# The last 96 columns of gate and up as one product with tokens stationary, transposed by DMA

## Chip, cores, metric

One core of one Trainium2 chip. The metric is the device time of one execution in microseconds (us), the median of several runs; lower is better. The span in a profile (first to last instruction) is about 1.8 us shorter than the time of the same run. All runs quoted here are fast (none over 1.5% above the fastest run of its kernel).

Engines: PE is TensorE (matmuls), PEld its weight loads, DVE is VectorE, ACT is ScalarE, POOL is GpSimd, SP is the engine that issues most DMAs.

## The reference, cut

Two layers, each a linear attention block and a gated MLP ("GLU"), on 2048 tokens of width 512, hidden width F = 1376. The change touches the GLU alone:

```python
def _B_ref(x, W_gate, W_up, W_down):              # W_gate, W_up: 512 x 1376, W_down: 1376 x 512
    gate = jnp.einsum("bsd,df->bsf", x, W_gate)
    up = jnp.einsum("bsd,df->bsf", x, W_up)
    gate = gate * (lambda x, dt: x.astype(dt))(gate > 0, gate.dtype)
    h = gate * up
    return jnp.einsum("bsf,fd->bsd", h, W_down)
...
x = x + _A_ref(_layernorm(x, axis=-1), A_wqkv, A_w_phi, A_wo)
x = x + _B_ref(_layernorm(x, axis=-1), B_W_gate, B_W_up, B_W_down)
# and both once more
```

## The kernel before

A recording layer notes each operation with what it reads and writes and a guessed duration; a list scheduler orders the operations of each engine, trying several priorities; each DMA gets one of 48 completion semaphores in rotation. 1376 = 10 x 128 + 96, so each GLU has eleven chunks of hidden columns. In all of them the weights are the stationary operand (loaded before the matmul, PEld) and the tokens stream against them, so that the result has hidden columns on partitions, as the down product needs it. The tokens go through in slabs: two slabs of 256 and three of 512 tokens in each layer.

```python
S, D, H, DH, F = 2048, 512, 32, 16, 1376
NT, NSLAB, NC, NFC = 16, 4, 4, 11
FLAST = F - 10 * 128                       # 96
...
def glu_up(self, ts, ring, tag, out, on_act=()):      # ts: the slab's tiles of 128 tokens
    ...
    def step(fc):
        Mf = 128 if fc < 10 else FLAST
        ...
        for bank, W, wr in ((gb, k.Wg, "Wg"), (ub, k.Wu, "Wu")):
            for ic in range(NC):
                op("pe", ... e.matmul(k.pb[bank][0:Mf, 0:n], W[:, ic, fc * 128:fc * 128 + Mf],
                                      k.yT[:, ic, c0:c0 + n], ...) ...)
        op("act", ... e.activation(k.gate_sb[0:Mf, gs, 0:n], k.pb[gb][0:Mf, 0:n], ACT.Relu) ...)
        ...                                           # in some chunks ACT also copies up to SBUF
        op("dve", ... e.tensor_tensor(k.hT[0:Mf, u, 0:n], k.gate_sb[...], ..., ALU.mult) ...)
    for fc in range(NFC):
        out.append(lambda fc=fc: step(fc))
```

Normalised tokens come to yT (all but the first four tiles), and attention outputs to oT, by DMA transposes on the SP queue. Two pieces of the recording layer matter later: how completion semaphores are handed out, and the waits at the very end.

```python
def prepare(self):
    ...
    dma_rr = 0
    for o in order:
        ...
        if o.is_dma:
            stream = ("d", dma_rr % self.n_dma_sems)      # 48 semaphores in rotation
            dma_rr += 1
...
def final_dma_waits(self, eng, dma_sems):                 # on SP, after its last DMA
    for s, c in self.final_counts.items():
        if isinstance(s, tuple) and c:
            eng.wait_ge(dma_sems[s[1]], 16 * c)
```

The softmax here doesn't subtract the row's maximum and nothing guards it: scores larger than these inputs give would overflow.

Of the kernel before, what the change touches and what calls it, by code (L numbers as in the profile page):

```python
# [347 lines left out]
ALU = mybir.AluOpType  # L348
# [20 lines left out]
class Kernel:  # L369
# [10 lines left out]
    def r(self, *key):  # L380
        x = self.R.get(key)
        if x is None:
            x = self.R[key] = Res(str(key), pe_ordered=(key[0] == "pb"))
        return x
# [12 lines left out]
    def alloc(self, E):  # L397
        nc = self.nc

        def sb(name, shape, dt=BF16):  # L400
            t = E(nc.sbuf_tensor(name, [P] + shape, dt))
            setattr(self, name, t)
            return t

        sb("x_sb", [NT, 512])
        sb("yT", [NC, S])
        sb("wv_p", [NC, 512])
        sb("Wqp", [NC, 512])
        sb("Wkp", [NC, 512])
        sb("wo_p", [NC, 512])  # L410
        sb("Wg", [NC, F])
        sb("Wu", [NC, F])
        sb("Wd", [NFC, 512])
        sb("expk", [NT, 2, 512])
        sb("vsb", [NT, NC, 130])
        sb("expq", [NSLAB, NC, 2, 512])
        sb("kvbd", [NG, GW])
        sb("hT", [NHU, 512])
        sb("numbf", [2, NG, GW])
        sb("tsc", [2, 1024])  # L420
        sb("osb", [2, 512])
        sb("oT", [4, NC, 128])
        sb("gate_sb", [3, 512])
        sb("ytile", [4, 512])
        sb("ident", [128])
        sb("mask8", [8])
        sb("mask8t", [8])
        sb("phi_c", [NC, DH])
        sb("stats6", [NT, 6], FP32)
        sb("mv", [NT, 2], FP32)  # L430
        sb("rv1", [NT, 1], FP32)
        sb("rstd", [NT, 1], FP32)
        sb("nmr", [NT, 1], FP32)
        sb("agg", [4, 3], FP32)
        sb("aggw", [2], FP32)
        sb("mhalf", [4, 1], FP32)
        sb("Zk", [2, 64], FP32)
        sb("rZk", [4, 64], FP32)
        sb("zm", [2, 64], FP32)
        sb("zd", [2, 32], FP32)  # L440
        sb("zr", [2, 32], FP32)
        sb("ab", [2, 64])
        self.ps = E(nc.psum_tensor("ps", [P, 8, 512], FP32))
        self.pb = [self.ps[:, i, :] for i in range(8)]
        self.RP = [self.r("pb", i) for i in range(8)]


    def setup(self):
        op, dma, r = self.op, self.dma, self.r
        k = self  # L450
        A_wqkv, A_w_phi, A_wo = self.A_wqkv, self.A_w_phi, self.A_wo
        xv = self.A_x.rearrange("b (t p) d -> p (b t) d", p=P)
        wqkv_v = A_wqkv.rearrange("(c p) n -> p c n", p=P)
        WqT = k.hT[:, 4:8, :]
        wk_n = k.hT[:, 8:12, :]
        BD = k.hT[:, 12, :].rearrange("p (c m) -> p c m", c=NC)
        R_BD = r("hT", 12)
        R_WqT = [r("hT", i) for i in range(4, 8)]
        R_wkn = [r("hT", i) for i in range(8, 12)]

        ones_c = k.tsc[:, 0, 0:128]
        op("pool", lambda e: e.memset(ones_c, 1.0), [], [r("tsc", 0)], 200, "ones")
        op("pool", lambda e: e.affine_select(k.ident[:], ones_c, [[1, 128]], ALU.is_equal, 0.0, base=0, channel_multiplier=-1),
           [r("tsc", 0)], [r("ident")], 300, "ident")
        op("pool", lambda e: e.memset(k.mhalf[:], -0.5), [], [r("mhalf")], 150, "mhalf")
        op("pool", lambda e: e.affine_select(k.mask8t[:], ones_c[:, 0:8], [[-16, 8]], ALU.is_ge, 0.0, base=0, channel_multiplier=1),
           [r("tsc", 0)], [r("mask8t")], 200, "mask8 a")
        op("pool", lambda e: e.affine_select(k.mask8[:], k.mask8t[:], [[16, 8]], ALU.is_ge, 0.0, base=15, channel_multiplier=-1),
           [r("mask8t")], [r("mask8")], 200, "mask8 b")

        n0 = len(self.prog.ops)

        def ldx(t0, t1, after=()):
            dma("sp", lambda e: e.dma_start(k.x_sb[:, t0:t1, :], xv[:, t0:t1, :]), list(after), [r("x", t) for t in range(t0, t1)], 131072 * (t1 - t0) if t1 > t0 + 1 else 96000, f"dma x{t0}")
        dma("sp", lambda e: e.dma_start(k.phi_c[:], A_w_phi.rearrange("(kc hl) d f -> (hl d) kc f", hl=8)), [], [r("phi_c")], 16384, "dma phi")
        for ic in range(NC):
            dma("act", (lambda ic: lambda e: e.dma_start(wk_n[:, ic, :], A_wqkv[ic * 128:(ic + 1) * 128, 512:1024]))(ic), [], [R_wkn[ic]], 96000, f"dma wk{ic}")
        for t in range(4):
            ldx(t, t + 1)
        first = [R_wkn[3]]  # L480
        ldx(4, 8, first)
        dma("sp", lambda e: e.dma_start(k.wv_p[:], wqkv_v[:, :, 1024:1536]), first, [r("wv", ic) for ic in range(NC)], 524288, "dma wv")
        ldx(8, 12, first)
        ldx(12, 16, first)
        o = dma("sp", lambda e: e.dma_start_transpose(WqT, A_wqkv[:, 0:512]), first, R_WqT, 524288, "dma wqT")
        o.dur = 7000.0
        for j, o in enumerate(self.prog.ops[n0:]):
            o.boost = 1e9 - 1e7 * j

        op("pool", lambda e: e.tensor_tensor(  # L490
            BD.rearrange("p c (h f) -> p c h f", f=DH),
            k.phi_c[:].unsqueeze(2).to_broadcast([P, NC, 8, DH]),
            k.mask8[:].unsqueeze(1).unsqueeze(3).to_broadcast([P, NC, 8, DH]), ALU.mult),
           [r("phi_c"), r("mask8")], [R_BD], 1040, "BD")
        op("pool", lambda e: e.memset(k.aggw[:, 0:1], -0.5), [], [r("aggw")], 100, "agg w0")
        op("pool", lambda e: e.memset(k.aggw[:, 1:2], 1.0 / D), [], [r("aggw")], 100, "agg w1")
        op("pool", lambda e: e.memset(k.vsb[:, :, :, 128:130], 1.0), [], [r("vones")], 250, "v ones")
        op("pool", lambda e: e.tensor_copy(k.kvbd[:, :, 136:144], k.mask8[:].unsqueeze(1).to_broadcast([P, NG, 8])), [r("mask8")], [r("kvones")], 230, "kv ones")

    def compose_k(self):  # L500
# [242 lines left out]
    def glu_up(self, ts, ring, tag, out, on_act=()):  # L743
        op, r, k = self.op, self.r, self
        RY = [r("yT", t) for t in ts]
        c0, n = ts[0] * 128, len(ts) * 128
        du = n * 0.42 + 1
        def step(fc):
            Mf = 128 if fc < 10 else FLAST
            gb, ub = next(ring), next(ring)  # L750
            u = self.unit % NHU
            self.unit += 1
            for t in ts:
                self.unit_of[t, fc] = (u, (t - ts[0]) * 128)
            gs = u % 3
            for bank, W, wr in ((gb, k.Wg, "Wg"), (ub, k.Wu, "Wu")):
                for ic in range(NC):
                    op("pe", (lambda bank, W, ic, fc, Mf: lambda e: e.matmul(k.pb[bank][0:Mf, 0:n], W[:, ic, fc * 128:fc * 128 + Mf], k.yT[:, ic, c0:c0 + n], start=(ic == 0), stop=(ic == NC - 1)))(bank, W, ic, fc, Mf),  # L758
                       [r(wr, ic)] + RY, [self.RP[bank]], du, f"{tag} {wr} {ts[0]} {fc} {ic}")
            op("act", (lambda Mf, gb, gs: lambda e: e.activation(k.gate_sb[0:Mf, gs, 0:n], k.pb[gb][0:Mf, 0:n], ACT.Relu))(Mf, gb, gs),  # L760
               [self.RP[gb]], [r("gate", gs)], 170 + n * 0.833, f"{tag} relu {ts[0]} {fc}")
            if fc in on_act:
                tu = 12 + u % 4
                ru = [r("expk", tu, 0), r("phik", tu, 0)]
                op("act", (lambda Mf, ub, tu: lambda e: e.activation(k.expk[0:Mf, tu, 0, 0:n], k.pb[ub][0:Mf, 0:n], ACT.Copy))(Mf, ub, tu),  # L765
                   [self.RP[ub]], ru, 170 + n * 0.833, f"{tag} up {ts[0]} {fc}")
                op("dve", (lambda Mf, tu, gs, u: lambda e: e.tensor_tensor(k.hT[0:Mf, u, 0:n], k.gate_sb[0:Mf, gs, 0:n], k.expk[0:Mf, tu, 0, 0:n], ALU.mult))(Mf, tu, gs, u),  # L767
                   [r("gate", gs)] + ru, [r("hT", u)], 150 + n * 0.535, f"{tag} h {ts[0]} {fc}")
            else:
                op("dve", (lambda Mf, ub, gs, u: lambda e: e.tensor_tensor(k.hT[0:Mf, u, 0:n], k.gate_sb[0:Mf, gs, 0:n], k.pb[ub][0:Mf, 0:n], ALU.mult))(Mf, ub, gs, u),  # L770
                   [r("gate", gs), self.RP[ub]], [r("hT", u)], 150 + n * 1.04, f"{tag} h {ts[0]} {fc}")

        for fc in range(NFC):
            out.append(lambda fc=fc: step(fc))

    def glu_down(self, t, ring, tag, halves=1):
# [195 lines left out]
```

## Time and profile before

| | before |
|---|---|
| median time | 392.31 us (3 runs, 391.47 to 392.65) |
| span of the profile | 390.3 us |
| PE busy | 379.4 us (97%) |
| the chunk of 96 columns on PE | 80 matmuls, 13.9 us by start-to-start times |

From the page of the kernel before: span, busy time by engine, the two queues whose packets the page calls "instruction", here taken as instruction fetches (packets, MB, share of 16 DMA engines), and the engines' shares of the chain that ended last.

```profile
span 390.3 us, 6397 instructions
PE 379.4 (97%) x2331; PEld 208.0 (53%) x2331; DVE 272.0 (70%) x547; ACT 206.6 (53%) x389; POOL 168.5 (43%) x284
...
q8 instruction: 18, 0.29, 0.3%
q14 instruction: 13, 0.11, 0.1%
...
PE 88%; POOL 4%; ACT 3%; DMA 2%; DVE 1%; issue 1%; ACTq 0%; POOLq 0%
```

PE is the bound, and the chain that ended last, on the page below, says the same. Where it has slack is seen by stretches. These are the busy times by window (columns: window, its length, then busy us and count for PE, PEld, DVE, ACT, POOL, granted clock, DMA share, GB/s); the first and last stretch hold the two GLUs:

```profile
72.00:223.00 151.00, 150.88 (x839) 80.04 (x840) 111.31 (x224) 64.03 (x132) 66.78 (x111) 1.00 0.18 35
262.00:378.00 116.00, 116.00 (x660) 62.59 (x659) 64.45 (x140) 54.63 (x120) 30.03 (x62) 1.00 0.19 41
```
```profile
240.00:265.00 25.00, 24.57 (x180) 14.75 (x180) 21.26 (x53) 21.58 (x38) 14.22 (x30) 1.00 0.24 49
```

PE is busy for all but 0.1 us of the two long stretches, so PE time removed there should come off the time. Between 240 and 265 us, where the attention of the second layer goes over into its GLU, 0.4 us is idle even by busy time. Busy time hides small gaps, because the record of a matmul (379 ns for 512 columns) is longer than its step (216 ns). Later sections therefore use "gaps": the start-to-start times of all matmuls, less what each shape takes when nothing is in the way: 216, 109, 62.5 and 56 ns for 512, 256, 144 and up to 129 columns, by the steps in the trace before, and for 192 columns the 83 ns of the forecast.

The groups of matmuls by shape (count, busy us, mean ns, idle before), the chunk first, and below it two shapes with few columns:

```profile
L758 PE MATMUL ps<-yT,Wu 128*96 128x512 bf16 x24 | 9.1, 379 | 0.0
L758 PE MATMUL ps<-yT,Wg 128*96 128x512 bf16 x24 | 8.9, 379 | 0.0
L758 PE MATMUL ps<-yT,Wu 128*96 128x256 bf16 x16 | 3.6, 273 | 0.0
L758 PE MATMUL ps<-yT,Wg 128*96 128x256 bf16 x16 | 3.3, 273 | 0.0
...
L706 PE MATMUL ps<-kvbd,expq 128*128 128x144 bf16 x256 | 35.0, 226 | 0.5 <-ACT numbf L366 0.5
L663 PE MATMUL ps<-vsb,expk 128*128 128x129 bf16 x256 | 19.9, 220 | 1.0 <-POOL expk L634 0.6 <-ACT expq L693 0.3
```

"128*96" says that 96 of the array's columns hold weights; the other chunks have 128*128. All tokens stream all the same: the median step is 216 ns for 512 tokens and 109 for 256 with either form, so the 32 empty columns save no time.

### The profile page before, as it was taken

What the parts mean: (1) busy time and instruction counts of PE and PEld (TensorE: products, weight loads), DVE (VectorE), ACT (ScalarE), POOL (GpSimd) and SP (SyncE); (2) the same over time, 40 slices, a digit from 0 to 9 for tenths busy, and PEclk for the clock granted to TensorE, in tenths of its full rate; (3) what the DMA queues carried; (4) which work ended last, traced back from release to release, by engine and by line L of the source; (5) the groups of instructions that cost most, each with busy time, mean ns of one, the idle gap of its engine ahead of it and who ended that gap; (6) DMA issues with size and microseconds to landing.
All of it is one profiled execution on the core that took longest, in us unless ns stands there. A gap on an engine that the chain in (4) does not pass through costs nothing.

```text
span 390.3 us, 6397 instructions
## 1 busy us (share of the span) xinstructions
PE 379.4 (97%) x2331; PEld 208.0 (53%) x2331; DVE 272.0 (70%) x547; ACT 206.6 (53%) x389; POOL 168.5 (43%) x284
## 2 busy tenths in 40 slices
PE   5999989999999999999999999999999999999997
PEld 3445554667644544444444457567774554444444
DVE  4999978877766888866766777897986776232222
ACT  5898859834633404533453484985563462553340
POOL 5499936641724363372244543584553242100000
DMA  6833682311311322401000110132323132100002
GB/s 179 228 67 71 191 299 53 69 40 32 53 40 27 43 55 44 84 10 28 14 15 0 27 29 3 40 80 57 55 55 69 27 42 67 29 14 27 17 12 67
DMA packets 61663, 23.01 MB, mean 59 GB/s; under 512 B 53472, under 2 KB 60608, under 8 KB 61632
## 3 DMA queue, kind: packets, MB, share of 16 engines
q1 hardware_dynamic: 60912, 22.02, 24.4%
q10 hardware_dynamic: 720, 0.59, 0.5%
q8 instruction: 18, 0.29, 0.3%
q14 instruction: 13, 0.11, 0.1%
HBM read 7.91 MB, written 2.10 MB: 26 GB/s over the span
## 4 chain that ended last, share of the span: by engine, by line
PE 88%; POOL 4%; ACT 3%; DMA 2%; DVE 1%; issue 1%; ACTq 0%; POOLq 0%
PE ps L758 39%; PE ps L785 19%; PE ps L617 7%; PE ps L737 7%; PE ps L690 6%; PE ps L706 4%; PE ps L663 3%; PE ps L648 2%; POOL expk L634 2%; ACT expq L693 2%; DVE stats L551 1%; DMA x_sb<-in_A_x_dram 1%; DMA hT<-in_A_wqkv_dram 1%; ACT expk L620 1%; POOL rstd L576 1%
## 5 line engine op out<-in xcount | busy, mean ns | idle before, releaser
L758 PE MATMUL ps<-yT,Wg 128*128 128x512 bf16 (+3 forms) x440 | 130.1, 337 | 0.5 <-DMA yT<-ytile 0.2
L758 PE MATMUL ps<-yT,Wu 128*128 128x512 bf16 (+3 forms) x440 | 129.6, 336 | 0.0
L760 ACT ACTIVATE gate_sb<-ps 128x512 bf16<-128x512 f32 (+3 forms) x110 | 55.9, 512 | 105.3 <-PE ps L758 102.9
L785 PE MATMUL ps<-Wd,hT 128*128 128x512 bf16 (+2 forms) x363 | 106.8, 373 | 0.0
L634 POOL TENSOR_TENSOR expk<-expk,rZk 128x1024 bf16<-128x1024 bf16 (+1 forms) x32 | 59.5, 1878 | 37.1 <-DVE rZk L631 19.7
L758 PEld LDWEIGHTS ps<-yT,Wg 128*128 128x128 bf16 (+1 forms) x440 | 43.4, 100 | 33.8 <-issue 1.1
L758 PEld LDWEIGHTS ps<-yT,Wu 128*128 128x128 bf16 (+1 forms) x440 | 43.7, 100 | 32.6 <-ACT expk L765 0.2
L767 DVE TENSOR_TENSOR hT<-gate_sb,expk 128x512 bf16<-128x512 bf16 (+3 forms) x73 | 29.8, 409 | 37.9 <-ACT expk L765 33.0
L785 PEld LDWEIGHTS ps<-Wd,hT 128*128 128x128 bf16 (+1 forms) x363 | 35.3, 98 | 36.6 <-DVE x_sb L787 0.6
L551 DVE BATCH_NORM_STATS2 stats<-x_sb 128x6 f32<-128x512 bf16 x64 | 42.6, 682 | 5.5 <-DMA x_sb<-in_A_x_dram 5.1
L366 ACT ACTIVATE numbf<-ps 128x432 bf16<-128x432 f32 x64 | 33.1, 536 | 19.5 <-PE ps L706 19.4
L629 DVE TENSOR_REDUCE Zk<-expk 128x64 f32<-128x1024 bf16 x32 | 37.7, 1194 | 5.7 <-ACT expk L620 5.4
L731 POOL TENSOR_TENSOR osb<-tsc 128x512 bf16<-128x512 bf16 x28 | 32.5, 1162 | 19.9 <-DVE tsc L726 17.8
L737 PE MATMUL ps<-wo_p,oT 128*128 128x512 bf16 x128 | 39.8, 379 | 0.0
L770 DVE TENSOR_TENSOR hT<-gate_sb,ps 128x512 bf16<-128x512 bf16 (+2 forms) x37 | 22.7, 613 | 20.8 <-PE ps L758 19.6
L693 ACT ACTIVATE expq<-ps 128x1024 bf16<-128x1024 f32 (+1 forms) x40 | 32.6, 861 | 7.3 <-PE ps L690 7.0
L765 ACT ACTIVATE expk<-ps 128x512 bf16<-128x512 f32 (+3 forms) x73 | 36.1, 497 | 0.1
L706 PE MATMUL ps<-kvbd,expq 128*128 128x144 bf16 x256 | 35.0, 226 | 0.5 <-ACT numbf L366 0.5
L620 ACT ACTIVATE expk<-ps 128x512 bf16<-128x512 f32 x44 | 23.9, 598 | 21.5 <-PE ps L617 21.2
L690 PE MATMUL ps<-yT,Wqp 128*128 128x512 bf16 x128 | 34.6, 379 | 0.6 <-ACT expq L693 0.5
L787 DVE TENSOR_TENSOR x_sb<-x_sb,ps 128x512 bf16<-128x512 bf16 (+1 forms) x33 | 22.0, 669 | 18.8 <-PE ps L785 18.4
L559 POOL TENSOR_TENSOR rstd<-rv,mhalf 128x1 f32<-128x1 f32 (+1 forms) x53 | 31.9, 607 | 2.9
(73 smaller groups left out, 429.2 us busy)
## 6 DMA issues: line engine op xcount, KB each, us to landing
out_dram<-x_sb SPq DMA_DIRECT2D x15, 128.0 KB, 1.7
x_sb<-in_A_x_dram SPq DMA_DIRECT2D x3, 512.0 KB, 6.2
Wu<-in_B_W_up_dram SPq DMA_DIRECT2D x4, 344.0 KB, 5.9
Wg<-in_B_W_gate_dram SPq DMA_DIRECT2D x4, 344.0 KB, 5.5
Wd<-in_B_W_down_dram SPq DMA_DIRECT2D x5, 256.0 KB, 6.9
yT<-ytile SPq DMA_TRANSPOSE x60, 2.5
hT<-in_A_wqkv_dram ACTq DMA_DIRECT2D x4, 128.0 KB, 3.1
x_sb<-in_A_x_dram SPq DMA_DIRECT2D x4, 128.0 KB, 3.7
```

The lines of the kernel that those rows point to most:

```text
L366: return e.activation(out, in_, ACT.Copy) if hasattr(e, "activation") else e.tensor_copy(out, in_)
L551: op("dve", (lambda t: lambda e: e.bn_stats(k.stats6[:, t, :], k.x_sb[:, t, :]))(t), [r("x", t)], [r("st", t)], 685, f"{tag} stats {t}")
L629: op("dve", lambda e: e.tensor_reduce(k.Zk[:, zb, :], k.expk[:, t, :, :].rearrange("p s (h f) -> p (s h) f", f=16), AX.X, ALU.add), [r("ex ...
L634: op(eng, (lambda s0, s1: lambda e: e.tensor_tensor(k.expk[:, t, s0:s1, :].rearrange("p s (h f) -> p (s h) f", f=16), k.expk[:, t, s0:s1, ...
L690: op("pe", (lambda c, ic, bank: lambda e: e.matmul(k.pb[bank][:], k.Wqp[:, ic, c * 128:(c + 1) * 128], k.yT[:, ic, st * 512:(st + 1) * 512 ...
L693: op("act", (lambda c0, s, b0: lambda e: e.activation(k.expq[:, st, c0:c0 + w, s, :], k.ps[:, b0:b0 + w, :], ACT.Exp, scale=(1.0 - 2.0 * s ...
L706: op("pe", (lambda s, c, j, g0, bank: lambda e: e.matmul(k.pb[bank][:, j * GW:(j + 1) * GW], k.expq[:, st, c, s, tt * 128:(tt + 1) * 128], ...
L737: op("pe", (lambda c, bank: lambda e: e.matmul(k.pb[bank][:], k.oT[:, ob, c, :], k.wo_p[:, c, :], start=(c == 0), stop=(c == NC - 1)))(c, ...
L758: op("pe", (lambda bank, W, ic, fc, Mf: lambda e: e.matmul(k.pb[bank][0:Mf, 0:n], W[:, ic, fc * 128:fc * 128 + Mf], k.yT[:, ic, c0:c0 + n] ...
L760: op("act", (lambda Mf, gb, gs: lambda e: e.activation(k.gate_sb[0:Mf, gs, 0:n], k.pb[gb][0:Mf, 0:n], ACT.Relu))(Mf, gb, gs), [self.RP[gb] ...
L765: op("act", (lambda Mf, ub, tu: lambda e: e.activation(k.expk[0:Mf, tu, 0, 0:n], k.pb[ub][0:Mf, 0:n], ACT.Copy))(Mf, ub, tu), [self.RP[ub] ...
L785: op("pe", (lambda fc, Kf, u, c0, bank, m0, m1: lambda e: e.matmul(k.pb[bank][:, m0:m1], k.hT[0:Kf, u, c0:c0 + 128], k.Wd[0:Kf, fc, m0:m1] ...
```

## The change

The chunk's gate and up weights are put side by side, 192 columns, and streamed against a stationary tile of 128 tokens. A tile then needs 4 matmuls of 192 columns instead of a share of 8 that stream 128 tokens each (768 instead of 1024 columns). The product comes out with tokens on partitions, so it has to be transposed: by DMA, one transpose for each slab. To hide that, this chunk is first in each slab.

```diff
-        sb("Wg", [NC, F])
-        sb("Wu", [NC, F])
+        sb("Wgu", [NC, 2, F])
+        self.Wg, self.Wu = self.Wgu[:, :, 0, :], self.Wgu[:, :, 1, :]
...
+        sb("h10t", [4, 128])
...
+        op("pool", lambda e: e.memset(k.h10t[:], 0.0), [], [r("h10t")], 900, "h10t zero")
...
-            Mf = 128 if fc < 10 else FLAST
+            Mf = 128
...
-        for fc in range(NFC):
+        def last():
+            fc, m = NFC - 1, len(ts)
+            b0, b1 = next(ring), next(ring)
+            pv = k.ps[:, b0:b0 + 2, :].rearrange("p b (c m) -> p (b c) m", c=2)
...
+            for j, t in enumerate(ts):
+                for ic in range(NC):
+                    op("pe", ... e.matmul(pv[:, j, 0:2 * FLAST]..., k.yT[:, ic, t * 128:(t + 1) * 128],
+                                          k.Wgu[:, ic, :, F - FLAST:F], ...) ..., 84, ...)
+            op("act", ... e.activation(gv, pv[:, 0:m, 0:FLAST], ACT.Relu) ...)
+            op("dve", ... e.tensor_tensor(k.h10t[:, 0:m, 0:FLAST], gv, pv[:, 0:m, FLAST:2 * FLAST], ALU.mult) ...)
+            self.dma_tr(... e.dma_start_transpose(k.hT[:, u, 0:n]..., k.h10t[:, 0:m, :]...) ...)
+
+        out.append(last)
+        for fc in range(NFC - 1):
             out.append(lambda fc=fc: step(fc))
```

More of the change, by code (lines that the diff above doesn't have):

```diff
@@ L771, in step @@
                    [r("gate", gs), self.RP[ub]], [r("hT", u)], 150 + n * 1.04, f"{tag} h {ts[0]} {fc}")
-        for fc in range(NFC):
+        def last():
+            fc, m = NFC - 1, len(ts)
+            b0, b1 = next(ring), next(ring)
+            pv = k.ps[:, b0:b0 + 2, :].rearrange("p b (c m) -> p (b c) m", c=2)
+            u = self.unit % NHU
+            self.unit += 1
+            gs = u % 3
+            for j, t in enumerate(ts):
+                self.unit_of[t, fc] = (u, j * 128)
+                for ic in range(NC):
+                    op("pe", (lambda t, j, ic: lambda e: e.matmul(pv[:, j, 0:2 * FLAST].rearrange("p (a f) -> p a f", a=2), k.yT[:, ic, t * 128:(t + 1) * 128], k.Wgu[:, ic, :, F - FLAST:F], start=(ic == 0 and j % 2 == 0), stop=(ic == NC - 1), skip_group_check=True))(t, j, ic),
+                       [r("Wg", ic), r("Wu", ic), r("yT", t)], [self.RP[(b0, b1)[j // 2]]], 84, f"{tag} gu {t} {fc} {ic}")
+            RB = [self.RP[b0], self.RP[b1]] if m > 2 else [self.RP[b0]]
+            gv = k.gate_sb[:, gs, 0:m * FLAST].rearrange("p (j f) -> p j f", j=m)
+            op("act", lambda e: e.activation(gv, pv[:, 0:m, 0:FLAST], ACT.Relu), RB, [r("gate", gs)], 170 + m * FLAST * 0.833, f"{tag} relu {ts[0]} {fc}")
+            op("dve", lambda e: e.tensor_tensor(k.h10t[:, 0:m, 0:FLAST], gv, pv[:, 0:m, FLAST:2 * FLAST], ALU.mult),
+               [r("gate", gs)] + RB, [r("h10t")], 150 + m * FLAST * 1.04, f"{tag} h {ts[0]} {fc}")
+            self.dma_tr(lambda e: e.dma_start_transpose(k.hT[:, u, 0:n].rearrange("p (j q) -> p j q", j=m), k.h10t[:, 0:m, :].rearrange("p j f -> p (j f)")),
+                        [r("h10t")], [r("hT", u)], f"{tag} htr {ts[0]}")
+        out.append(last)
+        for fc in range(NFC - 1):
             out.append(lambda fc=fc: step(fc))
```

## The prediction

> **What bounds the kernel now.** TensorE. The page gives PE 379.4 of 390.3 us (97%), at a granted clock of 1.00; the chain of waits is 88% PE. Stretch by stretch, PE is busy 150.9 of 151.0 us from 72 to 223 us and 116.0 of 116.0 us from 262 to 378 us. They hold all of the GLU products. The start-to-start times of matmuls in the trace show no slack there: 216 ns for 512 columns, 109 for 256, 62-63 for 144, 56 for 129. Gaps outside: about 1.9 us between 57 and 72 us and 1.3 us between 223 and 262 us; the rest of the idle time is before 57 us.
>
> **What is removed.** The last chunk has 96 columns of gate and of up, with the weights stationary: 96 of the array's 128 columns filled, yet all tokens stream. By the groups by shape: 48 matmuls of 512 tokens and 32 of 256. By the start-to-start times: 48 x 0.216 + 32 x 0.109 = 13.9 us.
>
> **What is added on PE.** 128 matmuls (32 tiles x 4), tokens stationary, 192 columns streaming. The trace has no 192-column matmul; its four sizes fit 0.42 ns per column plus 2-3 ns, so I estimate 83 ns. [...] here 129-column matmuls step at 56 ns, each with a 128x128 load of its own, so loads should hide under 83 ns as well. 128 x 0.083 = 10.6 us. Net: **-3.2 us of PE time**.
>
> **What moves elsewhere.** ACT: the relu of this chunk covers 384 instead of 512 elements per slab, and the 8 copies of up in this chunk (588 and 375 ns each) go. DVE: the product reads PSUM in all ten slabs, by the 684 ns for 512 about 0.55 us (two tiles about 0.35), where eight took 424 or 288 before: about +1 us in all. SP queue: ten more transposes, 1.19 us to issue and about 2.5 us to land each (as the yT and oT ones); they are issued at the start of a slab, ten chunks before the down products read them, so they should hide. POOL: one memset in the setup, where POOL idles 1.3 us: nothing.
>
> **Critical path.** Nearly all of the 3.2 us lies on it, because PE is back to back exactly where the chunk stands, and no engine behind it is near its limit there (DVE 111 of 151 us, ACT 64). The scheduler re-orders everything after about 56 us, so the 3.2 us of gaps around the two attention stretches may change by half a microsecond or so either way.
>
> **Prediction:** 389.2 us, range 387.7 to 390.6. Chances: faster by over 2% 0.02, within 2% 0.96, slower by over 2% 0.02.
>
> **What would show it.** Right: PE busy time down by about 3 us; 192-column matmuls 82-86 ns start to start; the two GLU stretches still without PE gaps; no PE wait on the new transpose. Wrong steps: 192-column matmuls near 100 ns (weight loads not hidden) would eat 2 us; PE waits for hT from the transposes, or for yT/oT transposes queued behind them on SP, would show as new PE gaps; larger gaps at 57-72 or 223-262 us would be the scheduler's re-ordering.
>
> **What would make it wrong.** Re-ordering, or head-of-line blocking on SP: either could give back 1-3 us.

The 83 ns are worked out from the four measured steps alone, and 13.86 - 10.62 = 3.24 us is the -3.2 us of the forecast. The 1 to 3 us that re-ordering or blocking on SP "could give back" are not worked out from any measured number.

## The result

| | before | after |
|---|---|---|
| median time | 392.27 us (4 runs, 391.47 to 392.65) | 390.41 us (4 runs, 389.96 to 390.54) |
| ratio | | 0.995, 95% interval 0.9935 to 0.9964 |
| span of the profile | 390.3 us | 388.6 us |
| PE busy | 379.4 us | 375.3 us |
| column time of PE | 372.87 us | 369.64 us |

A ratio is the mean time of one kernel's fast runs over that of the other's in the same rounds, so not quite the ratio of the medians. Column time is the sum of the undisturbed steps named above over all matmuls. The measured gain is 1.9 us, where 3.2 us were forecast; the time lies in the forecast range, near its upper end.

The page after, the same lines:

```profile
span 388.6 us, 6472 instructions
PE 375.3 (97%) x2379; PEld 209.0 (54%) x2379; DVE 271.4 (70%) x547; ACT 201.4 (52%) x381; POOL 169.1 (44%) x285
...
q8 instruction: 19, 0.31, 0.3%
q14 instruction: 14, 0.11, 0.1%
...
PE 86%; POOL 4%; ACT 4%; DMA 3%; DVE 2%; issue 1%; SPq 0%; DVEq 0%; POOLq 0%
```

The two GLU stretches, which are now 0.3 and 0.0 us short of full:

```profile
72.00:223.00 151.00, 150.68 (x868) 80.71 (x866) 112.03 (x226) 62.95 (x130) 67.65 (x111) 1.00 0.21 39
262.00:378.00 116.00, 116.00 (x688) 63.34 (x686) 65.43 (x141) 52.65 (x117) 29.86 (x62) 1.00 0.20 46
```

The new matmuls, the only group of their line:

```profile
L785 PE MATMUL ps<-Wgu,yT 128*128 128x192 bf16 x128 | 16.8, 246 | 1.7 <-DMA yT<-ytile 1.7
```

Their start-to-start time has a median of 82 ns, and all 128 together step through 10.6 us. So the forecast of the PE term holds: 13.9 - 10.6 = 3.3 us by what was measured, and 3.23 us in the sum of column times. But this line also has what the chunk's four groups in the kernel before did not have, an idle time of 1.7 us, ended by a yT transpose. That is in the stretch from 240 to 265 us:

```profile
240.00:265.00 25.00, 23.11 (x174) 14.49 (x171) 20.36 (x51) 20.78 (x37) 14.28 (x30) 1.00 0.28 56
```

Here PE is idle 1.9 us, against 0.4 before. The waits of PE between 240 and 260 us, the long one of the changed kernel (who waited for whom, us, times, longest):

```profile
PE ps L785 <- DMA yT<-ytile: 1.7, 1, 1.7
```

For the same window the view lists no wait of PE in the kernel before. The order in time around the spot, before and then after (start us, us, instruction, and in brackets idle time and what ended it):

```profile
256.51 0.35 PE L706 MATMUL ps<-kvbd,expq 128*128 128x144 bf16 x3
256.70 1.03 PE L737 MATMUL ps<-wo_p,oT 128*128 128x512 bf16 x4
257.82 0.27 PE L758 MATMUL ps<-yT,Wg 128*128 128x256 bf16 x1
257.93 0.27 PE L758 MATMUL ps<-yT,Wu 128*128 128x256 bf16 x1
```

```profile
254.89 0.59 PE L739 MATMUL ps<-wo_p,oT 128*128 128x512 bf16 x2
255.32 0.49 PE L785 MATMUL ps<-Wgu,yT 128*128 128x192 bf16 x4
255.65 0.59 PE L739 MATMUL ps<-wo_p,oT 128*128 128x512 bf16 x2
257.93 0.51 PE L785 MATMUL ps<-Wgu,yT 128*128 128x192 bf16 x4 [1.69 <-DMA yT<-ytile]
258.27 1.47 PE L760 MATMUL ps<-yT,Wgu 128*128 128x256 bf16 x12
```

Before, four of the attention's wo products (L737) were followed by the first gate and up products after 0.26 us. After, the 192-column product of the first token tile runs at 255.32 us, two wo products follow, and the 192-column product of the second tile stands until 257.93 us. The chain that ended last goes through the same place:

```profile
252.86 0.31 POOL ab L724
253.17 0.28 POOL zm L719
253.44 4.44 DMA yT<-ytile
257.89 0.04 issue
```

The transpose issued at 253.44 us took 4.44 us to land. The view of DMA issues gives the usual time, as the median over each kind of transpose (count, us from issue to landing):

```profile
yT<-ytile SPq DMA_TRANSPOSE x60, 2.4
hT<-h10t SPq DMA_TRANSPOSE x10, 2.4
```

The spans of the two profiles differ by 1.65 us. The pieces, read from the two traces:

| piece | before | after | difference |
|---|---|---|---|
| first matmul starts | 3.23 | 3.36 | +0.13 |
| column time of PE | 372.87 | 369.64 | -3.23 |
| gaps before 80 us | 9.84 | 9.54 | -0.30 |
| gaps from 240 to 265 us | 1.21 | 2.41 | +1.20 |
| gaps elsewhere | 0.33 | 0.33 | 0.00 |
| last matmul's start to the end | 2.77 | 3.33 | +0.56 |

The first row and the gaps before 80 us are not the change's: over the 14 profiles taken here the latter range from 9.0 to 10.8 us, also between profiles of one and the same program (9.54 and 10.34 for the changed kernel). What took back the gain are two rows: the gaps at the start of the second GLU, and the tail.

### Two suspects

The tail. The last store lands 2.35 us after the last matmul's start before, and 2.32 us after; the difference comes later. SP, having issued its last store, goes through the waits for all 48 completion semaphores, mostly two at a time, one pair each 60 ns. This is a part of SP's instructions at the end of the two traces, before and then after (start us, duration ns, semaphores; 104 is the first of the 48):

```
last landing 389.84, on 104         last landing 387.60, on 114
389.470  +27  149 and 107           386.782  +28  141 and 115
389.532  +28  150 and 106           386.844 +779  142 and 114
389.591  +28  151 and 105           387.655  +28  143 and 113
389.854  +41  104                   ... seven more pairs ...
                                    388.138  +28  151 and 105
                                    388.205  +41  104
```

Before, the last store happened to have the semaphore that is waited for last (104). The change adds ten DMAs, so the rotation of 48 gives the last store another one (114), nine pairs from the end: they come after the landing, and cost 0.55 us.

The late transpose. The DMA packet records of the trace show, at 255.87 us, a 16 KB packet of queue 8, of kind "instruction", which took 929 ns. Queue 8 is taken as PE's instruction stream on two grounds: from one of its 16 KB packets to the next PE executes on average 254 (before) or 257 (after) instructions, single stretches 197 to 314; and increments put into PE's stream alone move it (experiments 2 and 5). The packets of the other such queue, 14, are of 8 KB at most, and which engines it serves was not looked into. Between 252 and 258 us the records have 32 packets of 4 bytes before the landing of each transpose. For the transpose before the late one they all start between 254.05 and 254.28 us. For the late one, 30 of 32 start between 255.36 and 255.60 us, in good time, but the last two at 256.79 and 256.80 us, just when the fetch packet ends (255.87 + 0.93), and the landing is counted at 257.89 us. So 15 pairs are in time and one is late; what held that one up the records do not show, since they name no DMA engine. Why the landing comes another 1.1 us after the last pair stays open.

That this is not one odd transfer is seen from all SBUF-to-SBUF transposes after 60 us in the 14 profiles:

| an instruction packet of at least 8 KB within 2.5 us after the issue | transposes | median us to landing | 90% below | over 2.7 us |
|---|---|---|---|---|
| no | 914 | 2.42 | 2.50 | 12 |
| yes | 276 | 3.08 | 4.11 | 161 |
| of these, one of 16 KB (queue 8, PE's) | 144 | 3.78 | 4.23 | 114 |
| of these, only of 8 KB (queue 14) | 132 | 2.52 | 3.27 | 47 |

After a late transpose the issue of the next one on the SP queue often takes longer too: where SP issues a transpose within 0.1 us after the issue of another, the issue takes a median of 1.27 us (272 cases), but 2.09 us (19 cases) when that other one took over 3.5 us to land.

This is an association over many places; the experiments have to show that the fetch is the cause, and that it explains the gap. The rivals: the new product stands too early in the slab ("first"), or the ten new transposes hold up others on the SP queue.

### The profile page after: what moved, and what is told of

It is laid out like the page before. It is cut to its first block, busy times and chain, and to the rows that moved or that the text cites. A ratio compares the mean times of both kernels' runs of the same rounds, so it can differ in the third digit from the quotient of the medians.

```text
span 388.6 us, 6472 instructions
## 1 busy us (share of the span) xinstructions
PE 375.3 (97%) x2379; PEld 209.0 (54%) x2379; DVE 271.4 (70%) x547; ACT 201.4 (52%) x381; POOL 169.1 (44%) x285
## 4 chain that ended last, share of the span: by engine, by line
PE 86%; POOL 4%; ACT 4%; DMA 3%; DVE 2%; issue 1%; SPq 0%; DVEq 0%; POOLq 0%
PE ps L760 35%; PE ps L808 19%; PE ps L619 7%; PE ps L739 6%; PE ps L692 5%; PE ps L650 4%; PE ps L708 4%; PE ps L665 3%; PE ps L785 3%; POOL expk L636 1%; DMA yT<-ytile 1%; DMA x_sb<-in_A_x_dram 1%; DMA oT<-osb 1%; ACT expk L622 1%; POOL rstd L561 1%; DVE stats L553 1%
## 5 line engine op out<-in xcount | busy, mean ns | idle before, releaser
L760 PE MATMUL ps<-yT,Wgu 128*128 128x512 bf16 (+1 forms) x800 | 177.9, 337 | 0.0
L760 PEld LDWEIGHTS ps<-yT,Wgu 128*128 128x128 bf16 x800 | 76.9, 98 | 60.6 <-ACT expk L767 1.2
L762 ACT ACTIVATE gate_sb<-ps 128x512 bf16<-128x512 f32 (+1 forms) x100 | 50.8, 513 | 82.6 <-PE ps L760 67.6
L769 DVE TENSOR_TENSOR hT<-gate_sb,expk 128x512 bf16<-128x512 bf16 (+1 forms) x65 | 28.2, 435 | 29.4 <-ACT expk L767 24.6
L767 ACT ACTIVATE expk<-ps 128x512 bf16<-128x512 f32 (+1 forms) x65 | 32.4, 499 | 1.4 <-PE ps L760 1.2
L560 POOL TENSOR_SCALAR rv<-mv 128x1 f32<-128x1 f32 (+1 forms) x53 | 12.7, 242 | 46.7 <-DVE mv L555 46.5
L561 POOL TENSOR_TENSOR rstd<-rv,mhalf 128x1 f32<-128x1 f32 (+1 forms) x53 | 30.7, 583 | 3.3
L596 DVE TENSOR_SCALAR ytile<-x_sb,mv,rstd 128x512 bf16<-128x512 bf16 x52 | 23.1, 447 | 12.0 <-POOL rstd L561 11.5
L772 DVE TENSOR_TENSOR hT<-gate_sb,ps 128x512 bf16<-128x512 bf16 (+1 forms) x35 | 21.3, 609 | 13.3 <-PE ps L760 10.5
```

Of the source, the lines that this page charges most:

```text
L561: op("pool", lambda e: e.tensor_tensor(k.rstd[:, t0:t1, :], k.rv1[:, t0:t1, :], k.mhalf[:, 0:n], ALU.pow), [r("rv1", t) for t in ts] + [r( ...
L760: op("pe", (lambda bank, W, ic, fc, Mf: lambda e: e.matmul(k.pb[bank][0:Mf, 0:n], W[:, ic, fc * 128:fc * 128 + Mf], k.yT[:, ic, c0:c0 + n] ...
L762: op("act", (lambda Mf, gb, gs: lambda e: e.activation(k.gate_sb[0:Mf, gs, 0:n], k.pb[gb][0:Mf, 0:n], ACT.Relu))(Mf, gb, gs), [self.RP[gb] ...
```

## The experiments

Three chips, each measured in five rounds with the kernel before on the same chip: before 391.56 us in the first (9 runs), 392.00 in the second (11), 392.15 in the third (9). All outputs were correct.

### 1. The tail: only the rotation of semaphores shifted

Edit, in the changed kernel with `first` = 0 and in the kernel before with `first` = 24 (the semaphore waited for first). The order of all instructions stays.

```diff
-        dma_rr = 0
+        dma_rr = (first + 1 - sum(o.is_dma for o in ops)) % self.n_dma_sems
```

> The changed kernel with only the rotation of DMA completion semaphores shifted, so that its last store uses the semaphore that the final run of waits on the sync engine reaches last (as in the kernel before). The order of all instructions stays the same. Theory of the tail: after the last store's landing nine more pairs of waits follow at 60 ns each in the changed kernel, none in the kernel before; so this run should be 0.5 us faster than the changed kernel (about 389.9 against 390.4), with the last landing to the end of the span down from 1.0 to about 0.45 us. Rival (the longer tail is chance of the store's landing): no change.

> The kernel before with the same shift the other way: its last store uses the semaphore that is waited for first. Theory of the tail: all 24 following pairs of waits come after the landing, 24 x 0.06 = 1.4 us slower than the kernel before (ratio about 1.0036). Rival: no change (1.000).

Measured: the changed kernel with its tail mended 389.13 us, ratio 0.9933 (0.9921 to 0.9946); the kernel before with its tail spoilt 392.88 us, ratio 1.003 (1.0017 to 1.0042), 1.3 us over 391.56. In the profiles, last landing to SP's last wait is 0.02 us in the first (387.25 to 387.27) and 1.49 us in the second (389.33 to 390.82), and last matmul's start to the end 2.77 and 4.24 us. The theory of the tail holds in both directions: what this kernel, with its 48 completion semaphores, pays after its last store depends on which of them that store has. The changed kernel itself was not in this call, so its gain of 0.55 us is read from the profiles; the times in the same rounds follow in experiment 4.

### 2. Shift PE's instruction fetches in the changed kernel

Edit: 104 increments of a semaphore that nobody reads, one before a matmul, in the gate and up products of the last two slabs of the first GLU. The estimate was that they cost PE nothing there and that every later fetch then comes 104 instructions earlier in the work.

```diff
+            if e == "pe" and o.name.startswith(("B1 Wg 8 ", "B1 Wu 8 ", "B1 Wg 12 ", "B1 Wu 12 ")) and self.pad > 0:
+                eng.sem_inc(self.padsem)
+                self.pad -= 1
             ins = o.fn(eng)
```

> The changed kernel with 104 increments of an unused semaphore put into the TensorE stream of the third and fourth slab of the first GLU, one before a matmul[...]. They shift every later instruction fetch of TensorE[...] by 104 instructions. Theory of the fetch: the fetch packet at 255.9 us no longer falls on the yT transpose that the first gate/up product of the second GLU waits for; this transpose lands in 2.4 instead of 4.4 us, the PE gap of 1.85 us there shrinks to under 0.5 us, and the time falls by 1.3 to 1.8 us, to about 388.8. Rivals: if the gap comes from putting the 192-column product first, or from the queue of transposes on the sync engine, the gap and the time stay (390.4).

Measured: 389.65 us, ratio 0.9945 (0.9932 to 0.9957), not to be told from the changed kernel's 0.995; the expected 388.8 us was missed. The profile says why. The fetch moved from 255.87 to 247.04 us; the yT transpose now landed in 2.49 us, and the gap at 257.93 us is gone. But at its new place the packet fell on an oT transpose (issued 245.10, landed 249.03 us, 3.93 us), and the gap moved with it: 1.01 us before the wo product at 249.08 us. The waits of PE between 240 and 262 us:

```profile
PE ps L744 <- DMA oT<-osb: 0.8, 1, 0.8
```

The gaps from 240 to 265 us fell from 2.41 to 1.63 us. The increments cost no PE time: the gaps between 80 and 240 us and after 265 us are 0.33 us, as without them. So the fetch moved the gap, as expected, and the size was missed, because the place was badly chosen.

### 3. The same with 92 increments, and the tail mended

Edit: 104 becomes 92, so that the packet falls between two transposes; and the edit of experiment 1 with `first` = 0.

> The changed kernel with 92 instead of 104 increments, and with its last store's semaphore waited for last. The 12 instructions between 104 and 92 move the TensorE fetch from 247.0 to about 248.0 us, into a stretch where no transpose is in flight. Theory of the fetch: both the gap of 1.85 us (changed kernel) and that of 1.0 us (with 104) are gone, PE gaps between 240 and 260 us sum to 0.6 us instead of 2.4 us. With the 0.5 us of the tail the time is about 388.2 on the scale where the changed kernel is 390.4 (ratio to the kernel before about 0.989 to 0.990, that is the full 3.2 us of the removed columns and some more). Rivals (order of the products, queue of transposes): the gap stays somewhere, ratio 0.993 as with the tail alone.

Measured: 387.95 us, ratio 0.990 (0.9886 to 0.9914). The fetch came at 246.69 us. The gaps from 240 to 265 us are 0.65 us, and no transpose issued between 244 and 262 us took more than 2.50 us. (One issued at 262.21 us took 5.07 us, with the next fetch at 263.97 us, but PE did not stand for it.) The product stands first in the slab, as in the changed kernel, and the SP queue has the same transposes in the same order; only twelve instructions that do nothing distinguish the fetch's place from that of experiment 2. The edit of the tail, which is new here too, left the gap where it was in experiment 1 (gaps of 2.10 us from 240 to 265 us). That decides against both rivals as causes of this gap.

### 4. All on one chip

> The changed kernel unaltered, on one chip with the next two, so that the three can be compared in the same rounds. Expected ratio to the kernel before 0.995, with the PE gap in front of the 192-column product near 257 us again[...], 1.5 to 1.9 us.

> The changed kernel with its last store's semaphore waited for last, again. Theory of the tail: 0.5 us under the unaltered changed kernel of the same rounds. Rival (chance of the first measurement): no difference.

> The version with both the tail mended and the 92 increments, again. Theory of the fetch: 1.3 to 1.8 us under the version with the tail alone in the same rounds; both parts together about 2 us under the changed kernel, ratio to the kernel before about 0.990.

| | median us | ratio to before, 95% | gaps before 80 us | gaps 240 to 265 us | last matmul to end |
|---|---|---|---|---|---|
| changed kernel | 390.01 | 0.9947 (0.9932 to 0.9963) | 10.34 | 2.09 | 3.34 |
| tail mended | 389.18 | 0.9920 (0.9907 to 0.9932) | 9.31 | 2.35 | 2.77 |
| tail and fetch | 388.27 | 0.9894 (0.9879 to 0.9909) | 10.24 | 0.63 | 2.75 |

The order is as expected. The tail's step is 0.83 us in the times, where 0.5 was expected and the profiles show 0.57. The wait at the 192-column product is there again in the two without the increments (1.53 and 1.79 us), late by a fetch packet at 256.19 and 255.00 us. The step from the second to the third row is 0.9 us in the times, less than the expected 1.3 to 1.8, while the gaps from 240 to 265 us fall by 1.72 us; in these two profiles the gaps before 80 us, where the programs do not differ, went the other way by 0.93 us. Such chance is in each run, so the times alone size the step only to about half a microsecond; this pair (0.9920 to 0.9894) and the pair of experiments 1 and 3 (0.9933 to 0.990) together give about 1.1 us. The gaps from 240 to 265 us are steadier: in all four profiles of the changed order without increments they are 2.09 to 2.41 us, and in two of the order before (the second is that of the spoilt tail) 1.21 and 1.29 us.

The version with both, in time around the former wait, and its window. The lines have moved by five; L790 is the 192-column product:

```profile
255.46 0.59 PE L744 MATMUL ps<-wo_p,oT 128*128 128x512 bf16 x2
255.89 0.49 PE L790 MATMUL ps<-Wgu,yT 128*128 128x192 bf16 x4
256.22 0.59 PE L744 MATMUL ps<-wo_p,oT 128*128 128x512 bf16 x2
256.65 0.49 PE L790 MATMUL ps<-Wgu,yT 128*128 128x192 bf16 x4
256.98 1.53 PE L765 MATMUL ps<-yT,Wgu 128*128 128x256 bf16 x12
```

```profile
240.00:265.00 25.00, 24.80 (x188) 15.75 (x186) 21.80 (x55) 21.43 (x40) 14.55 (x31) 1.00 0.29 58
```

The two tiles' products (255.89 and 256.65 us) follow the wo products without a gap, and PE is busy 24.8 of 25.0 us.

### 5. The kernel before, with a fetch pushed onto its transposes

Edit as in experiment 2, in the kernel before, with 68, then 44, then 54 increments. The aim was each time the yT transpose of the second tile, in flight from about 255.3 to 257.7 us.

> The kernel before with 68 such increments in the same slabs, which moves its TensorE fetch at 261.5 us to about 257.3 us, onto the landing of the same yT transpose. Theory of the fetch: that transpose lands about 2 us late, a PE gap of 1.2 to 2 us opens before the first gate/up product of the second GLU, and the time rises by 0.8 to 1.8 us (ratio 1.002 to 1.005). Rivals: no change.

> The kernel before with 44 increments instead of 68, to put the fetch, which fell at 253.7 us with 68 and at 261.5 us with none, at about 257 us, while the yT transpose of the second tile is in flight. Theory of the fetch: this transpose lands 1.5 to 2 us late, the PE gap in front of the first gate/up product of the second GLU grows to 1.5 to 2.2 us, the time rises by about 1 us (ratio 1.002 to 1.004). If the fetch misses the transpose, no verdict. Rivals: no change although the fetch hits.

> The kernel before with 54 increments; 44 put the fetch at 259.2 us and 68 at 253.7 us, so 54 should put it near 257 us, on the yT transpose of the second tile (in flight from 255.3 to 257.7 us). Theory of the fetch: that transpose lands 1.2 to 2 us late, the PE gap in front of the first gate/up product of the second GLU grows from 0.26 to about 1.5 to 2 us, and the time rises by 0.6 to 1.5 us (ratio 1.0015 to 1.004). If the fetch hits it and neither gap nor time grow, the theory falls.

| increments | fetch at us | what it hit | its landing took | gaps 240 to 265 us | median us, ratio (95%) |
|---|---|---|---|---|---|
| none | 261.52 | oT, issued at 259.62 us | 3.98 us | 1.21 | 391.56 to 392.15 |
| 68 | 253.68 | oT issued at 251.82 us, yT of the first tile | 4.00 and 3.06 us | 1.54 | 392.02, 1.0008 (0.9994 to 1.0023) |
| 44 | 259.21 | oT issued at 257.43 us | 3.98 us | 2.12 | 392.48, 1.0016 (1.0004 to 1.0028) |
| 54 | 259.53 | the same oT, issued at 257.65 us | 4.03 us | 2.17 | 392.82, 1.0018 (1.0005 to 1.0030) |

The aim was missed three times: the fetch's place does not move evenly with the count, by 7.8 us for 68 increments, but at the same spot for 44 and for 54. With 68 the times show nothing, but the profile does: PE stood 0.99 us before the first gate and up product, at 257.77 us (0.26 us in the kernel before). The view names no DMA for this wait, but in both kernels the product starts 0.09 us after the landing of the second tile's yT transpose. That transpose took the usual 2.48 us, but two late ones stood before it on the SP queue: the issue of the first tile's took 1.92 us instead of 1.19, so the second was issued 1.97 us after the first instead of 1.24 us. A nearby gap of 0.31 us went, so that the sum rose by 0.33 us only. The other two, though on another transpose than intended, show the effect in a kernel that has nothing of the change: that oT transpose, issued at 257.26 us and landed in 2.41 us in the kernel before, takes 4 us, and PE stands for it. With 54 increments:

```profile
260.57 0.27 PE L763 MATMUL ps<-yT,Wg 128*128 128x256 bf16 x1
261.72 0.61 PE L742 MATMUL ps<-wo_p,oT 128*128 128x512 bf16 x2 [0.87 <-DMA oT<-osb]
262.16 0.27 PE L763 MATMUL ps<-yT,Wg 128*128 128x256 bf16 x1
```

The time rises by 0.5 us (44) and 0.7 us (54) over the kernel before, both with an interval just above 1. The row without increments also shows that a hit need not cost anything: the oT transpose at 259.62 us was late by 1.6 us in the kernel before, and PE had other work in its order (a gap of 0.08 us).

### 6. The transposes alone

Edit, in the kernel before: after the first chunk of each slab, one spare transpose of the chunk's hT to a tile that nobody reads, ten in all; last store's semaphore as before.

```diff
+        def spare_tr():
+            u, m = self.unit_of[ts[0], 0][0], len(ts)
+            self.dma_tr(lambda e: e.dma_start_transpose(k.trd[:, 0:m, :], k.hT[:, u, 0:n]), [r("hT", u)], [r("trd")], ...)
...
             out.append(lambda fc=fc: step(fc))
+            if fc == 0:
+                out.append(spare_tr)
```

> The kernel before with only the ten transposes of the change, as spare ones that nobody waits for (first chunk of each slab, to a spare tile, on the same queue), and the last store's semaphore kept as before. If transposes are hidden, as predicted: ratio 1.000 within 0.002, PE gaps elsewhere as before apart from what the re-ordering and a fetch do. If the queue of transposes costs 1 us or more, gaps before yT or oT users grow and the ratio is 1.003 or more.

Measured: 391.62 us, ratio 0.9993 (0.9981 to 1.0005). The gaps from 240 to 265 us are 1.28 us. The view of DMA issues has the spare ones with the usual time:

```profile
trd<-hT SPq DMA_TRANSPOSE x10, 2.4
```

The spare transposes cost nothing that these runs can tell (by the interval, at most 0.2 us), as predicted.

### 7. The product last in the slab

Edit, in the changed kernel with the tail mended: `out.append(last)` moved behind the loop over the other ten chunks. The scheduler then re-orders the whole rest.

> The changed kernel with the 192-column product last instead of first in each slab, and the last store's semaphore waited for last. Theory: removed columns are the same, so PE's own time is the same as in the changed kernel; but the transpose and its 2.4 us, with relu and product about 4 us from the last 192-column matmul to hT, now stands in front of the down products, above all in the last slab where PE has the least other work: 0 to 3 us slower than the changed kernel with the tail mended (389.1), by gaps at ends of slabs with a wait for the transpose to hT. Rival (placing it first causes the gap at 258 us): this gap is gone and the kernel is about 1.3 us faster, 387.8.

Measured: 389.65 us, ratio 0.9936 (0.9923 to 0.9948); first in the slab with the tail mended has 0.9933 and 0.9920. The gap near 258 us is 0.33 us here, as the rival expected, but the time did not fall to its 387.8 us: gaps from 240 to 265 us sum to 1.35 us (the largest, 0.72 us at 244.87 us, is mostly a wait for DVE and not for a DMA), and those before 80 us to 10.75, of which some are new (0.53 us at 62.7 and 0.54 at 72.9 us). No wait for the new transpose appears on PE, even at the end of the kernel. So putting it last costs nothing certain and gains nothing certain; with another order, fetches can also fall elsewhere (the change itself moved one from 261.52 to 255.87 us), so this run alone cannot tell the cause of the gap. Experiment 3 does.

## Why the prediction was right, and where it was off

- "Net: -3.2 us of PE time": right. The 192-column matmuls step at 82 ns where 83 was estimated, with a 128x128 weight load before each whose own record is longer (98 ns), so the loads are hidden; and the column time fell by 3.23 us.
- "The two GLU stretches still without PE gaps": right but for 0.3 us at the edge: a wait for an oT transpose at 75.5 us, itself late (4.11 us) with a fetch at 72.40 us.
- Transposes "should hide": right for the new ones. PE never waited for them (waits for hT from a DMA do not appear after the setup), and ten spare ones alone gave a ratio of 0.9993.
- ACT, DVE, POOL: no engine behind PE became a bound. DVE's busy time went from 272.0 to 271.4 us, so the estimated +1 us is not seen in its sum; ACT's fell from 206.6 to 201.4 us; POOL idled 1.30 us before the block product of the setup and the memset fitted there.
- "The 3.2 us of gaps around the two attention stretches may change by half a microsecond or so either way": this step failed in size. From 240 to 265 us they grew by 1.20 us in the first profile, and by 0.9 us in the second. The prediction named re-ordering as the reason to watch; what the runs showed in its place is a PE instruction fetch on a transpose that PE was about to need. The order of the new kernel is not worse in itself: with the packet out of the way, these gaps are 0.6 us, half of what the kernel before has. The blocking on the SP queue that the prediction also named is seen too, but behind a transpose that a fetch made late (with 68 increments, an issue of 1.92 us instead of 1.19), and not from the ten added ones.
- Not in the prediction at all: the ten added DMAs turned the semaphore rotation, which lengthened the tail by 0.56 us in the profile.
- The sum: -3.2 us of PE time, about +1 us of gaps, +0.6 us of tail, and chance in the first 80 us, is about the measured -1.9 us. The 389.2 us forecast was 1.2 us too low, inside the range, by 0.2 us, because the range allowed for gains given back; that they were given back by a fetch and the tail, which the prediction did not name, was luck for the range. A version that mends both gives 388.27 us in rounds where the changed kernel has 390.01 and the kernel before 392.15.

## What to carry to other kernels

Here a ragged last chunk left 32 of 128 array columns empty; streaming its 192 columns against stationary tokens took 10.6 us of PE instead of 13.9, and the start-to-start times of other shapes sized that gain to 2%. The same reckoning can be tried where another kernel has such a chunk. A change of about 1% should then be checked against two things that no line of the diff shows: where the instruction-fetch packets of the busiest engine fall among transfers that are waited for at once, and what the final waits do after the last store. Here they took back 1.2 and 0.56 us of 3.2. When a gap ends with a DMA, compare that one transfer's time to landing with the median of its kind before blaming the order or the queue.
